# The down-projection in three products begins in block 10 instead of block 11

## The chip, the cores and the metric

The kernel runs on one core of a Trainium2 chip. The metric is the device time of one execution in microseconds (us). TensorE appears in the profile as PE (its weight loads as PEld), VectorE as DVE, ScalarE as ACT, GpSimd as POOL, SyncE as SP.

## The reference

Eight batches of an attention over a packed set of 32 rows, and then one gated feed-forward layer over all 4608 tokens:

```python
p_packed = sm_attn(p, k, v)                # 8 x 8 heads, 576 rows, 64 wide, 32 packed rows
out = sm_attn(q, p_packed, p_packed)
x = out.transpose(0, 2, 1, 3).reshape(4608, 512)
h = x @ w_in                               # 512 -> 2048
g = h * np.tanh(np.log1p(np.exp(h)))       # Mish
return g @ w_out                           # 2048 -> 512
```

## The kernel before

The work runs in blocks `t`, one for each batch `b` (8) and each slice `f` of 128 of the 2048 hidden columns (16), so that blocks 0 to 15 belong to batch 0. A block computes its slice of `h` for the 576 rows of its batch (the up-projection, line 858: twelve matmuls into two PSUM tiles `ps_h`), ACT applies Mish (line 880, and line 882 for the last 64 rows, kept apart in `g_rest`), and the down-projection adds the slice to four accumulators `acc`, one for each chunk `c` of 128 rows. Up to block 16 the down-projection runs one block behind: block `t` multiplies the slice of block `t - 1` (`dn`).

The matmul takes float operands in one call (line 920), which the trace lists as two matmuls per chunk, or operands that are split in two halves, `hi` and `lo`, of another type. Split operands need three products (lines 900 to 902). Which is taken in batch 0 is decided by the constant THREE:

```python
if b == 0 and f < THREE:
    nc.tensor.matmul(out=accs[c], lhsT=grp.act[:, cs], rhs=wo[f], ...)
else:
    down_one(accs[c], grp.g[0], grp.g[1], cs, f, f == 0, f == NF - 1)
```

From slice THREE on, `halves()` splits the activations right after Mish: ACT writes `hi` (line 892), DVE subtracts for `lo` (line 896), into a tile `g_pair`. `split_wo` does the same with a slice of w_out: ACT at line 132, DVE (the function that it returns as `bottom`) at line 135. With the three products a block of batch 0 also puts the down-projection of chunk 1 behind its up-projection; with floats it stands ahead of it.

During batch 0 three other things run beside this. First, the weights arrive as 64-bit words and are turned into floats: ACT (lines 726 and 727, in `words`), POOL (lines 728 and 731, in `words`), then DVE (lines 738 and 742, in `join`). Second, the attention of batch 1 advances a step at a time (`advance(gen)`): in blocks 9 and 10 the values (PE line 585), whose two results DVE normalises at line 292 into `pp`; then PE transposes `pp` (line 596), DVE copies the transpose into `ppT` (line 597), and PE multiplies it with the queries (line 490, called the match here). Third, in every odd block w_in is multiplied with `ppT` of batch 0 for the next two slices (line 757), and ACT and DVE split the product (lines 799 and 800).

What an attention step leaves for DVE is put in a list, `pending`, and written into DVE's order only when the next step begins (`flush`). In blocks 0 to 15 the order on every engine is that of the program; each engine works strictly through its own. From block 16 on a scheduler orders the engines other than PE, PE keeps the program's order.

Of the kernel before, what the change touches and what calls it, by code (L numbers as in the profile page):

```python
# [28 lines left out]
LOADS = {0: 1, 2: 1, 4: 1, 5: 1, 6: 1}  # L29
LATER = 12  # L30
FLOATS = 4
THREE = 11
FIRST_SLOTS = 2
TOGETHER = 2
IN_TURN = 9
# [10 lines left out]
def body(  # L46
# [57 lines left out]
    stg = ctx.enter_context(tc.tile_pool(name="stg", bufs=1, side="right"))  # L104
    KEPT = STB - FIRST_SLOTS - (NF - THREE)

    wo, wo_hi, wo_lo = {}, {}, {}

    def slot(dtype, name, first):
        tag, n = ("st_a", FIRST_SLOTS) if first else ("st_b", STB - FIRST_SLOTS)  # L110
        return stg.tile([P, 2, FC], dtype, name=name, tag=tag, bufs=n)
# [7 lines left out]
    def wo_slot(dtype, name, late):  # L119
        tag, n = ("wo_b", NF - THREE) if late else ("wo_a", THREE + 1)  # L120
        return wts.tile([P, DO], dtype, name=name, tag=tag, bufs=n)

    def split_wo(i, later=False):
        own = STB - (NF - THREE)
        if i >= THREE or i < own:
            pair = slot(F32R, "wo_pair", KEPT <= i < own)
            wo_hi[i], wo_lo[i] = pair[:, 0], pair[:, 1]
        else:
            wo_hi[i], wo_lo[i] = [
                wo_slot(F32R, f"wo_{x}", 2 * (i - own) + n < NF - THREE) for n, x in enumerate(("hi", "lo"))  # L130
            ]
        top = nc.scalar.copy(out=wo_hi[i], in_=wo[i])

        def bottom():
            return nc.vector.tensor_tensor(
                out=wo_lo[i], in0=wo[i], in1=wo_hi[i].bitcast(F32), op=ALU.subtract
            )

        if later:
            return bottom  # L140
        both = [top, bottom()]
        if i < THREE:
            for x in both:
                tc.keep_in_program_order(x)
# [559 lines left out]
    class Weight:  # L704
# [15 lines left out]
        def words(self):  # L720
            x = self.st.rearrange("p m (n t) -> p (m n) t", t=2)
            j, half = divmod(self.at, 2)
            self.r = stg.tile(
                [P, FC], I32, name="wround", tag=f"{('upper', 'lower')[half]}_{j % WB == 0}", bufs=1 if j % WB == 0 else WB - 1
            )
            nc.scalar.activation(out=self.dst, in_=x[:, :, 1].bitcast(F32), func=AF.Copy, scale=F64_SCALE)
            nc.scalar.activation(out=self.r, in_=x[:, :, 0].bitcast(U32), func=AF.Copy, scale=2.0 ** -29)
            nc.gpsimd.tensor_scalar(
                out=self.dst, in0=self.dst, scalar1=F64_HIGH, scalar2=-F64_HIGH, op0=ALU.min, op1=ALU.max
            )  # L730
            nc.gpsimd.tensor_scalar(
                out=self.r.bitcast(BF16).rearrange("p (x t) -> p x t", t=2)[:, :, 1], in0=self.dst,
                scalar1=0.0, scalar2=1.0, op0=ALU.mult, op1=ALU.mult,
            )

        def join(self):
            bits = self.dst.bitcast(I32)
            nc.vector.tensor_scalar(
                out=bits, in0=bits, scalar1=3, scalar2=None, op0=ALU.logical_shift_left,
            )  # L740
            yield
            nc.vector.tensor_tensor(out=bits, in0=bits, in1=self.r, op=ALU.add)
# [77 lines left out]
    def split(*srcs, in_order=False):  # L820

        hi, lo = split_tiles("r")
        for n, src in enumerate(srcs):
            h, l = (x.rearrange("p (f u t) -> p u f t", u=len(srcs), f=src.shape[1])[:, n] for x in (hi, lo))
            both = [
                nc.scalar.copy(out=h, in_=src),
                nc.vector.tensor_tensor(out=l, in0=src, in1=h.bitcast(F32), op=ALU.subtract),
            ]
            if in_order and n == 0:
                for x in both:  # L830
                    tc.keep_in_program_order(x)
        return hi, lo
# [211 lines left out]
    with tc.manual_schedule(engines={mybir.EngineType.PE}):  # L1044
# [57 lines left out]
        for t in range(n_groups + LAG):  # L1102
# [35 lines left out]
            if t == 0:  # L1138
# [10 lines left out]
                ahead.up_floats((0, 1), (1,))  # L1149
                words(6)  # L1150
                join(3)
            if t == THREE:
                bottom()
            elif t == 12:
                split_wo(t)
            if t == 12:
                bottom = split_wo(13, True)
# [74 lines left out]
            if grp:  # L1232
                if t >= NF:
                    grp.halves()
                if t == THREE - 1:
                    bottom = split_wo(THREE, True)
                if t <= 13 and t != 1:
                    words(WORDS.get(t, 2 * t + 9))
            if dn and dn.b % 2 == 1 and dn.f % 4 == 2:
                rest["g"] = split(dn.g_rest[0][dn.f // 4], dn.g_rest[1][dn.f // 4], in_order=(dn.b, dn.f) == (1, 2))  # L1240
            last = dn and dn.b % 2 == 1 and dn.f == NF - 1 and not final
# [49 lines left out]
```

## Time and profile before

| | |
|---|---|
| median of 3 executions | 725.13 us (724.68 to 725.22) |
| profiled execution | 726.51 us, of which the span from first to last instruction 724.8 us |
| PE busy | 714.1 us, 99% of the span |
| DVE, ACT, POOL busy | 424.8, 318.5, 73.6 us |
| granted TensorE clock | 0.996 of full speed (mean) |

The profiled execution has 1.7 us around its span and stands 1.4 us above the median. A busy share is a mean over the whole span: in the page's slices from 18 to 127 us, in which batch 0 runs, DVE is busy for eight to nine tenths.

### The profile page before, as it was taken

What the parts mean: (1) busy time and instruction counts of PE and PEld (TensorE: products, weight loads), DVE (VectorE), ACT (ScalarE), POOL (GpSimd) and SP (SyncE); (2) the same over time, 40 slices, a digit from 0 to 9 for tenths busy, and PEclk for the clock granted to TensorE, in tenths of its full rate; (3) what the DMA queues carried; (4) which work ended last, traced back from release to release, by engine and by line L of the source; (5) the groups of instructions that cost most, each with busy time, mean ns of one, the idle gap of its engine ahead of it and who ended that gap; (6) DMA issues with size and microseconds to landing.
All of it is one profiled execution on the core that took longest, in us unless ns stands there. A gap on an engine that the chain in (4) does not pass through costs nothing.

```text
span 724.8 us, 12806 instructions
## 1 busy us (share of the span) xinstructions
PE 714.1 (99%) x5112; PEld 559.3 (77%) x5112; DVE 424.8 (59%) x765; ACT 318.5 (44%) x719; POOL 73.6 (10%) x105
## 2 busy tenths in 40 slices
PE   8899999999999999999999999999999999999997
PEld 5455568778887788787887888887888878888885
DVE  4888899758636566546645566455574565433322
ACT  4687776545424344254342544342442524432221
POOL 0494832000000000000000000000000000000000
PEclk9999999999999999999999999999999999999999
DMA  9999963651213512235102442133102000010002
GB/s 225 283 297 237 324 105 82 117 97 43 34 45 64 105 33 33 71 61 100 30 5 83 73 91 33 59 63 70 33 1 73 1 2 1 0 59 1 1 1 73
DMA packets 187115, 56.35 MB, mean 78 GB/s; under 512 B 175024, under 2 KB 177328, under 8 KB 187056
## 3 DMA queue, kind: packets, MB, share of 16 engines
q1 hardware_dynamic: 183376, 47.14, 29.5%
q10 hardware_dynamic: 2336, 4.20, 1.6%
q0 software_dynamic: 1344, 4.20, 1.5%
q8 instruction: 40, 0.66, 0.4%
q14 instruction: 19, 0.16, 0.1%
HBM read 46.07 MB, written 9.44 MB: 77 GB/s over the span
## 4 chain that ended last, share of the span: by engine, by line
PE 92%; ACT 3%; DVE 2%; DMA 1%; SPq 1%; issue 1%; POOL 1%; POOLq 0%; DVEq 0%; ACTq 0%
PE ps_h L858 26%; PE acc L900 16%; PE acc L902 15%; PE acc L901 15%; PE ps_w L757 4%; PE acc L920 4%; PE ps_rest L900 2%; PE ps_rest L902 2%; PE ps_rest L901 2%; PE ps_h L490 2%; DMA q_t<-in_q_dram 1%; PE ps_h L569 1%; PE ps_s L490 1%; PE ps_a L549 1%; PE ps_h L870 1%
## 5 line engine op out<-in xcount | busy, mean ns | idle before, releaser
L880 ACT ACTIVATE g<-ps_h 128x256 f32<-128x256 f32 (+2 forms) x256 | 97.3, 384 | 256.6 <-PE ps_h L858 235.1
L858 PE MATMUL ps_h<-aT_hi,wp_hi 128*128 128x256 f32 x496 | 150.7, 304 | 0.0
L858 PE MATMUL ps_h<-aT_lo,wp_hi 128*128 128x256 f32 x496 | 146.6, 295 | 0.0
L858 PE MATMUL ps_h<-aT_hi,wp_lo 128*128 128x256 f32 x496 | 146.4, 295 | 0.0
L895 DVE CAST g_hi<-g 128x512 fp32r<-128x512 f32 x112 | 47.4, 424 | 166.5 <-ACT g L880 166.5
L858 PEld LDWEIGHTS ps_h<-aT_hi,wp_hi 128*128 128x128 f32 x496 | 93.6, 189 | 13.7 <-issue 4.7
L858 PEld LDWEIGHTS ps_h<-aT_lo,wp_hi 128*128 128x128 f32 x496 | 93.5, 189 | 11.0 <-issue 1.9
L858 PEld LDWEIGHTS ps_h<-aT_hi,wp_lo 128*128 128x128 f32 x496 | 93.6, 189 | 0.0
L900 PE MATMUL acc<-wo_hi,g_hi 128*128 128x512 f32 x224 | 90.4, 404 | 0.0
L900 PE MATMUL acc<-wo_pair,g_hi 128*128 128x512 f32 x224 | 89.0, 397 | 0.0
L901 PE MATMUL acc<-wo_lo,g_hi 128*128 128x512 f32 x224 | 88.5, 395 | 0.0
L902 PE MATMUL acc<-wo_pair,g_lo 128*128 128x512 f32 x224 | 88.4, 394 | 0.0
L902 PE MATMUL acc<-wo_hi,g_lo 128*128 128x512 f32 x224 | 88.3, 394 | 0.0
L901 PE MATMUL acc<-wo_pair,g_hi 128*128 128x512 f32 x224 | 88.2, 394 | 0.0
L896 DVE TENSOR_TENSOR g_lo<-g,g_hi 128x512 fp32r<-128x512 f32 x112 | 77.0, 687 | 6.8 <-DVE g_hi L895 0.5
L768 ACT CAST wp_hi<-ps_w 128x512 fp32r<-128x512 f32 x56 | 30.1, 591 | 66.4 <-PE ps_w L757 66.4
L900 PEld LDWEIGHTS acc<-wo_hi,g_hi 128*128 128x128 f32 x224 | 42.2, 189 | 21.1 <-issue 10.9
L900 PEld LDWEIGHTS acc<-wo_pair,g_hi 128*128 128x128 f32 x224 | 42.2, 188 | 10.9 <-issue 3.8
L902 PEld LDWEIGHTS acc<-wo_hi,g_lo 128*128 128x128 f32 x224 | 42.1, 188 | 9.8
L902 PEld LDWEIGHTS acc<-wo_pair,g_lo 128*128 128x128 f32 x224 | 42.1, 188 | 9.7
L901 PEld LDWEIGHTS acc<-wo_lo,g_hi 128*128 128x128 f32 x224 | 42.1, 188 | 4.6
L901 PEld LDWEIGHTS acc<-wo_pair,g_hi 128*128 128x128 f32 x224 | 42.1, 188 | 4.5
(162 smaller groups left out, 982.9 us busy)
## 6 DMA issues: line engine op xcount, KB each, us to landing
w_st<-in_moe_w_in_dram SPq DMA_DIRECT2D x16, 512.0 KB, 7.7
w_st<-in_moe_w_out_dram SPq DMA_DIRECT2D x16, 512.0 KB, 7.0
q_n<-in_q_dram SPq DMA_DIRECT2D x56, 144.0 KB, 3.1
v_n<-in_v_dram SPq DMA_DIRECT2D x56, 128.0 KB, 2.8
k_n<-in_k_dram SPq DMA_DIRECT2D x32, 144.0 KB, 3.1
out_dram<-o ACTq DMA_DIRECT2D x14, 256.0 KB, 2.0
k_n<-in_k_dram SPq DMA_DIRECT2D x96, 32.0 KB, 2.0
out_dram<-o POOLq DMA_DIRECT2D x12, 256.0 KB, 2.5
```

Source lines behind the costliest of these rows:

```text
L490: nc.tensor.matmul(out=ps[u][h * NP:(h + 1) * NP, :], lhsT=packT[u * D:(u + 1) * D, n:n + NP], rhs=xT[u * D:(u + 1) * D, h ^ g, :], start= ...
L549: nc.tensor.transpose(out=ps[:, j, :], in_=flat[:, g, first + j * P:first + (j + 1) * P], identity=ident)
L757: nc.tensor.matmul(out=ps[h * NP:(h + 1) * NP, :], lhsT=ppTb[row:row + D, g, h * NP:(h + 1) * NP], rhs=w[row:row + D], start=True, stop=Tr ...
L768: nc.scalar.copy(out=hi, in_=ps)
L858: nc.tensor.matmul(out=ps, lhsT=w[:, fs], rhs=a[:, g, cs], start=(n == 0), stop=(n == 5))
L880: nc.scalar.activation(out=self.act[:, a:a + m], in_=ps[:, :m], func=AF.Mish)
L895: nc.vector.tensor_copy(out=hi, in_=self.act)
L896: nc.vector.tensor_tensor(out=lo, in0=self.act, in1=hi.bitcast(F32), op=ALU.subtract)
L900: nc.tensor.matmul(out=acc, lhsT=hi[:, cs], rhs=wh, start=start, stop=False)
L901: nc.tensor.matmul(out=acc, lhsT=hi[:, cs], rhs=wl, start=False, stop=False)
L902: nc.tensor.matmul(out=acc, lhsT=lo[:, cs], rhs=wh, start=False, stop=stop)
L920: nc.tensor.matmul(out=accs[c], lhsT=grp.act[:, cs], rhs=wo[f], start=f == 0, stop=f == NF - 1)
```

## The change

THREE goes from 11 to 10, so that slice 10 of batch 0 is multiplied as three products instead of floats. Its w_out slice is split in time for that: the ACT half at the end of block 9, the DVE half at the start of block 10. The same split leaves block 26, where it stood. The activations of block 10 get an ACT copy and a DVE subtraction, and chunk 1 in block 10 moves behind the up-projection. The split of the w_out slice of the block ahead now stands behind `words` instead of ahead of it. Sizes of some rings of buffers follow from THREE (`KEPT`, `wo_slot`, `split_wo`).

```diff
-THREE = 11
+THREE = 10
...
-            if t == THREE:
+            if THREE <= t < 12:
                 bottom()
             elif t == 12:
                 split_wo(t)
...
                 if t >= NF:
                     grp.halves()
-                if t == THREE - 1:
-                    bottom = split_wo(THREE, True)
                 if t <= 13 and t != 1:
                     words(WORDS.get(t, 2 * t + 9))
+                if THREE - 1 <= t < 11:
+                    bottom = split_wo(t + 1, True)
```

On DVE, at the start of block 10 (`wo_797` is slice 10 of w_out, `wo_867` and `wo_870` are slices 11 and 12, `pp` is the normalised result of the attention's values):

```order
 L742 ISA wi_0_98<-wi_0_98,wround 128x1024
 L742 ISA wi_1_99<-wi_1_99,wround 128x1024
-L292 TENSOR_SCALAR pp<-ps_pp,rs 128x128 x2
+L135 TENSOR_TENSOR wo_pair<-wo_797,wo_pair 128x512
+L292 TENSOR_SCALAR pp<-ps_pp,rs 128x128
+L896 TENSOR_TENSOR g_pair<-g,g_pair 128x512
+L292 TENSOR_SCALAR pp<-ps_pp,rs 128x128
 L738 TENSOR_SCALAR wo_867<-wo_867 128x512
 L738 TENSOR_SCALAR wo_870<-wo_870 128x512
```

The second normalisation stood right behind the first; now the subtraction on block 10's activations stands between them. Behind these rows follow, before and after alike, the two joins at line 742 of the same two slices and the two copies into `ppT` at line 597.

On PE, in block 10 (`wo_752` is slice 9 of w_out, `acc_537` to `acc_540` are the four chunks; the row of line 585 is the second group of values). First the place behind the values:

```order
 L920 MATMUL acc_537<-wo_752,g 128x512
 L585 MATMUL ps_pp<-v_n,a1T_n 32x64 x20
+L858 MATMUL ps_h_90<-aT_hi,wp_hi 128x256
+L858 MATMUL ps_h_90<-aT_lo,wp_hi 128x256
+L858 MATMUL ps_h_90<-aT_hi,wp_lo 128x256
```

The up-projection of block 10 (twelve matmuls, three are shown) now follows the values directly; before, chunk 1 (`acc_538`) stood between them and now stands behind the up-projection. Then the end of block 10 and the start of block 11, before:

```order
 L920 MATMUL acc_539<-wo_752,g 128x512
 L596 MATMUL ps_ppT<-ident,pp 128x128 x2
 L920 MATMUL acc_540<-wo_752,g 128x512
-L490 MATMUL ps_s_1148<-xT,ppT 32x288 x4
-L490 MATMUL ps_s_1149<-xT,ppT 32x288 x4
-L920 MATMUL acc_537<-wo_797,g 128x512
```

and with the change, from the match on:

```order
+L490 MATMUL ps_s_1154<-xT,ppT 32x288 x4
+L490 MATMUL ps_s_1155<-xT,ppT 32x288 x4
+L900 MATMUL acc_537<-wo_pair,g_pair 128x512
+L901 MATMUL acc_537<-wo_pair,g_pair 128x512
+L902 MATMUL acc_537<-wo_pair,g_pair 128x512
```

The match keeps its place behind the fourth chunk of slice 9; what follows it, the first chunk of slice 10, is now three matmuls. The order on POOL and SP is the same as before.

## Rows read from the trace of the kernel before

**Rows 1.** The page, busy time, share of the span and instructions of each engine.
```profile
PE 714.1 (99%) x5112; PEld 559.3 (77%) x5112; DVE 424.8 (59%) x765; ACT 318.5 (44%) x719; POOL 73.6 (10%) x105
```

**Rows 2.** Waits of PE from 45 to 719 us (total, times, longest).
```profile
PE ps_pp L585 <- DVE wp_lo L800: 0.4, 1, 0.4
```

**Rows 3.** Chain that ended last, blocks 10 to 12: start, us, what.
```profile
89.16 1.06 PE acc L920 x2
90.22 1.59 PE ps_h L858 x12
...
92.66 0.22 PE ps_ppT L596 x2
...
93.74 0.65 PE ps_s L490 x16
94.39 1.06 PE acc L920 x2
...
97.03 0.86 PE acc L920 x2
97.89 0.59 PE ps_w L757 x16
98.48 1.91 PE acc L920 x4
100.39 0.65 PE ps_s L490 x16
101.04 0.43 PE acc L900
101.47 0.23 PE acc L901
```

**Rows 4.** Timeline of DVE: start, us, what, times [idle before <-releaser].
```profile
85.71 1.69 DVE L738 TENSOR_SCALAR wi<-wi 128x512 int32<-128x512 int32 x2
87.32 2.19 DVE L742 CUSTOM_DVE_ANT_0 wi<-wi,wround 128x1024 uint16<-128x1024 uint16 x2
89.44 0.60 DVE L292 TENSOR_SCALAR pp<-ps_pp,rs 128x128 f32<-128x128 f32 x2
89.96 0.79 DVE L738 TENSOR_SCALAR wo<-wo 128x512 int32<-128x512 int32 x2
90.67 1.28 DVE L742 CUSTOM_DVE_ANT_0 wo<-wo,wround 128x1024 uint16<-128x1024 uint16 x2
92.81 0.49 DVE L597 COPY ppT<-ps_ppT 128x128 f32<-128x128 f32 x2 [0.86 <-PE ps_ppT L596]
```

**Rows 5.** Timeline of DVE, splits in blocks 12 and 13.
```profile
104.75 0.69 DVE L896 TENSOR_TENSOR g_pair<-g,g_pair 128x512 fp32r<-128x512 f32 x1
105.35 0.68 DVE L135 TENSOR_TENSOR wo_pair<-wo,wo_pair 128x512 fp32r<-128x512 f32 x1
...
109.73 1.24 DVE L896 TENSOR_TENSOR g_pair<-g,g_pair 128x512 fp32r<-128x512 f32 x1 [0.64 <-ACT g_pair L892]
```

**Rows 6.** Timeline of ACT, blocks 10 and 13.
```profile
92.22 0.62 ACT L132 CAST wo_pair<-wo 128x512 fp32r<-128x512 f32 x1
92.73 0.68 ACT L726 ACTIVATE wi<-w_st 128x512 f32<-128x512 f32 x1
...
109.08 0.62 ACT L892 CAST g_pair<-g 128x512 fp32r<-128x512 f32 x1
```

**Rows 7.** Timeline of POOL, blocks 9 to 11: last instruction, next after an idle stretch, last.
```profile
89.06 1.08 POOL L731 TENSOR_SCALAR wround<-wo 128x512 bf16<-128x512 f32 x1
93.50 0.61 POOL L728 TENSOR_SCALAR wi<-wi 128x512 f32<-128x512 f32 x1 [3.36 <-ACT wi L726]
...
97.93 1.08 POOL L731 TENSOR_SCALAR wround<-wo 128x512 bf16<-128x512 f32 x1
```

**Rows 8.** Windows: busy us of PE, PEld, DVE, ACT, POOL (instructions), granted clock, DMA share, GB/s.
```profile
20.00:24.00 4.00, 2.33 (x30) 1.46 (x34) 1.83 (x5) 2.95 (x7) 1.72 (x2) 0.86 1.02 395
24.00:44.00 20.00, 19.42 (x86) 9.44 (x75) 15.66 (x26) 15.57 (x32) 13.39 (x16) 0.94 0.95 300
```

## The prediction

> **What bounds the kernel now.** I read the page first: PE is busy for 714.1 of 724.8 us [rows 1]. Since a busy PE is not a PE at its peak, the second view is who PE waits for: from 45 to 719 us it waits once, for 0.4 us, in block 9 [rows 2]. The third is the chain that ended last, which through blocks 10 to 12 is one PE piece after the other, without a gap [rows 3]. So two things follow for any edit behind 45 us. PE work that goes is won in full, and an idle stretch that PE gains is lost in full, because no later wait is there to swallow it. The fourth view is therefore the order of time on DVE, ACT and POOL around block 10 [rows 4 to 7]: what matters there is whether something comes too late for PE.
>
> **The change, part by part.** The sum is made against the profiled execution (726.51 us), and its difference is then put on the median of 725.13 us, which is 1.4 us lower; nothing in the sum depends on that offset.
>
> *PE work.* Slice 10 in floats costs its four chunks 1.06 us (behind the match), 0.86 us and 1.91 us for the last two: 3.83 us [rows 3]. A product of halves takes 0.23 us, the first one behind a match 0.43 us [rows 3]. Twelve products with such a first one in two places (behind the match and, as the float pair of 1.91 us shows with its 0.19 us over 2 x 0.86, behind the weight product of line 757) are 2 x 0.43 + 10 x 0.23 = 3.16 us. PE saves 0.67 us. Moving chunk 1 in block 10 changes no work: the extra 0.2 us that a float chunk pays behind matmuls on parts of the array (1.06 against 0.86 us) is paid by the up-projection instead, for which I take 0.15 us, between 0 and 0.2.
>
> *Split of w_out's slice 10.* One ACT copy and one DVE subtraction go from block 26 to blocks 9 and 10. In block 26 nothing is won, since PE doesn't wait there [rows 2]. A few splits of batch 1 also change places with their neighbours, with the same cover. In block 9 the ACT copy (0.62 us [rows 6]) falls into an idle stretch that ends when the up-projection's results come. On DVE the subtraction comes first in block 10, at 89.44 us; it takes 0.6 us as long as POOL is idle (104.75 to 105.35) and about 1.2 us when POOL works (the 1.24 us row) [rows 5]. POOL works until 90.14 us [rows 7], so I take 0.95 us. It ends at 90.4 us and delays the first normalisation by as much, for which PE has until 92.66 us [rows 3].
>
> *Split of block 10's activations, and what queues behind it.* This is the term that decides. Before, both normalisations ran at 89.44 us, 0.26 us each, and were done at 89.96 us [rows 4]. Now the second stands in DVE's order behind the subtraction of line 896, which needs ACT's copy, which needs Mish, which needs the up-projection. The up-projection starts where chunk 1 stood, at 89.16 instead of 90.22 us, with the 0.15 us above: 0.91 us earlier. The ACT instruction behind Mish started at 92.22 us [rows 6], so the copy for `hi` starts at 91.31 us, takes 0.62 us, and DVE starts 0.03 us after it, as 109.08 + 0.62 against 109.73 us shows [rows 5, 6]: 91.96 us. With 0.60 us for the subtraction and 0.26 us for the normalisation DVE reaches the joins of lines 738 and 742 at 92.82 us, against 89.96 us before: 2.86 us late.
>
> *The four joins.* Between them and PE's match stand two instructions of line 738 and two of line 742, and then the copy into `ppT`. Their price has two values in the trace. With POOL idle they took 89.96 to 91.95 us, 1.99 us; with POOL at work 85.71 to 89.44 us, 3.73 us [rows 4]. Before, they ran in POOL's idle stretch from 90.14 to 93.50 us. Now they don't: ACT's conversion of the next weights starts 0.51 us behind the copy, at 91.82 us, and POOL follows 0.77 us after it (92.73 against 93.50) [rows 6, 7], at 92.6 us, and then works for 5.5 us (93.50 to 99.01) [rows 7]. So I take 3.73 us, with 1.99 us as the other end. The copies into `ppT` start at 96.55 us, the first takes about 0.3 us, and the match starts at about 96.9 us on the scale on which it started at 93.74 us [rows 3].
>
> What the Trainium skill says on this would make it longer: "SBUF — State Buffer", section Who interferes with whom, has DVE and GpSimd hold a shared pair of ports for a whole instruction, the other blocked. Taken strictly, with each of the four behind one POOL instruction of some 0.85 us, that would be 1.99 + 4 x 0.85 = 5.4 us and a match 1.7 us later still. The trace has the same four instructions under an unbroken run of POOL work in 3.73 us, so the row decides, and the strict reading has no more than a part of the 0.04 left for other cases below; it would end at 729.3 us.
>
> *PE at that place.* Values until 89.16, up-projection 1.74, chunks 1 and 2 0.86 each, transposes 0.22 (the second must wait for the normalisation until 92.85 us, some 0.2 us), chunk 3 0.86 us: PE reaches the match at 93.9 us and idles for 3.0 us. The match is 3.16 us late. From there on the saving of 0.67 us is won, and the net is 3.16 - 0.67 = **+2.5 us**, 727.6 us. With the joins at 1.99 us it is +0.75 us.
>
> *What is late next.* DVE is then about as late as PE, and both go on in the same order. The next meeting is the second match (100.39 us before), which needs the splits of line 800. After POOL's work ends (about 98.1 us) DVE's joins run at the short price again, so I count no second wait, and up to 0.4 us for one in the range. Later, slack is as before, since PE and DVE move together.
>
> **The rivals.**
>
> *The clock falls.* An idle stretch of 3.0 us may cost more than itself. In the window from 20 to 24 us PE was busy for only 2.33 of 4 us, and the granted clock fell below full speed in it and behind it: 0.86 there and 0.94 over the next 20 us [rows 8]. That is 0.14 x 4 + 0.06 x 20 = 1.8 us of full-speed clock lost. The same again gives +4.3 us, 729.4 us. Against it: PE is densely busy on both sides of the stretch here, and not there. That a clock falls when PE idles is also what the Trainium skill states ("TensorE: Matmul & The Clock Gate", Part 1); the two levels are 1.2 and 2.4 GHz, and the trace agrees that there is such a fall.
>
> *The joins run at the short price.* If POOL starts later than I count, or the joins slip through between its instructions, the net is +0.75 us, 725.9 us: no difference that a measurement of this kernel can tell, for which I take 0.2%, 1.45 us.
>
> *No wait.* If DVE gets the second normalisation done before it must wait for ACT, or ACT's part is much faster, PE finds `ppT` ready and the change gives its 0.67 us: 724.5 us. It would be won from where the copies into `ppT` start before 93.6 us, less than 0.8 us behind the normalisation at 92.82 us. Four instructions stand there that never took under 1.99 us [rows 4], and an order on DVE that is strict speaks against it. A gain over 0.2% would need 0.8 us more from nowhere that I can see.
>
> **How the numbers follow.** The wait without a fall of the clock: 0.47, own range 726.9 to 728.3 (0.4 us for a second wait, 0.3 us for POOL's and ACT's times either way). With the fall: 0.27, 728.5 to 730.2. Short joins: 0.12. No wait: 0.10. Something else, either side: 0.04. The time given is that of the first. A range from 725.6 to 729.9 us leaves out the case without a wait, part of the short joins and the top of the second, below 0.2 in all. Slower by over 0.2%: 0.76; within: 0.21 (short joins, no wait); faster: 0.03.
>
> **What would show it.** In the changed profile: no PE wait behind 45 us but one of some 3 us at line 490 near 94 us, released by DVE line 597 (the chain passes there from PE to DVE, through lines 738, 742 and 896, and to ACT's line 892); the two joins at some 0.9 to 1.2 us each instead of 0.4 and 0.7; POOL's idle stretch ending about 1 us earlier; twelve matmuls of lines 900 to 902 in block 11, and 3.2 us for them. If the granted clock shows a stretch at half behind 96 us, the first rival holds. I am wrong if PE goes through the match of block 10 without a wait, or if the wait is there and a later one gets shorter by it.

## The result and the profile after

| | before | after |
|---|---|---|
| median, 4 executions each, same chip | 725.17 us (724.68 to 726.56) | 730.11 us (729.93 to 731.85) |
| after/before | | 1.007, 95% interval 1.005 to 1.0091 |
| profiled execution, span | 726.51, 724.8 us | 730.13, 728.4 us |

The change makes the kernel slower by 4.94 us, 0.7%. The prediction was 727.6 us with a range to 729.9 us: the sign was right, the size was too small by 2.5 us, and the result lies 0.2 us above the range.

The page first, as [rows 1] before: busy us, share of the span, instructions of each engine.

```profile
PE 714.3 (98%) x5116; PEld 560.5 (77%) x5116; DVE 425.9 (58%) x766; ACT 319.7 (44%) x720; POOL 74.2 (10%) x105
```

PE has four matmuls more (the floats were 4 chunks of 2, the products are 12), DVE and ACT one instruction more each. Nothing in it tells of 5 us. The waits of PE from 45 to 719 us do, as [rows 2] before: us in total, times, longest.

```profile
PE ps_s L490 <- DVE ppT L597: 2.6, 1, 2.6
PE ps_pp L585 <- DVE wp_lo L800: 0.4, 1, 0.4
PE ps_ppT L596 <- DVE pp L292: 0.3, 1, 0.3
PE ps_w L757 <- DVE wo L738: 0.2, 1, 0.2
```

The second row was there before. The first is the predicted wait, the third the predicted 0.2 us ahead of the transposes; the fourth is new and was not predicted. Now the chain that ended last, through the same blocks as [rows 3]: start, us, what.

```profile
87.13 0.83 PE ps_pp L585 x40
87.96 1.80 PE ps_h L858 x12
89.77 0.02 issue
89.79 0.38 ACT g L880
90.17 0.12 ACT g_rest L882
90.29 0.55 ACT g_pair L892
90.83 0.02 issue
90.86 0.69 DVE g_pair L896
91.55 0.26 DVE pp L292
91.81 1.49 DVE wo L738 x2
93.29 2.12 DVE wo L742 x2
95.42 0.21 DVE ppT L597
95.63 0.04 issue
95.67 1.38 PE ps_s L490 x16
97.06 0.72 PE acc L900
97.78 0.43 PE acc L901
...
103.43 0.65 PE ps_s L490 x16
```

Before, all of this was PE. Now the chain leaves PE behind the up-projection, goes through ACT's Mish and copy to DVE's subtraction, the second normalisation and the four joins, and comes back to PE at the match: 5.9 us of it, from 89.77 to 95.67 us, are not PE's. The rows behind the idle stretch show something else. The match takes 1.38 us and a product 0.43 us; before they took 0.65 and 0.23 us [rows 3]. The windows of PE say why (length, busy us of PE, PEld, DVE, ACT, POOL with instructions, granted clock, DMA share, GB/s):

```profile
20.00:24.00 4.00, 2.65 (x31) 1.41 (x32) 2.91 (x7) 3.48 (x10) 2.02 (x3) 1.00 1.04 394
...
88.00:96.00 8.00, 5.09 (x28) 2.94 (x36) 6.84 (x12) 5.45 (x11) 5.06 (x7) 0.99 0.53 84
96.00:99.00 3.00, 3.00 (x22) 1.79 (x14) 2.93 (x7) 0.00 (x0) 0.80 (x1) 0.50 0.35 55
99.00:104.00 5.00, 5.00 (x52) 3.18 (x50) 2.98 (x6) 3.48 (x9) 0.69 (x2) 0.98 1.08 172
```

From 96 to 99 us the granted clock is 0.50, the lower of the two levels, 1.2 GHz, right behind the stretch in which PE stood idle; then it is back. The fall that the kernel before showed from 20 to 24 us (0.86, [rows 8]) is not there in this execution.

DVE around the wait, as [rows 4] before (start, us, what, times, idle before), and POOL, as [rows 7]:

```profile
88.24 1.20 DVE L135 TENSOR_TENSOR wo_pair<-wo,wo_pair 128x512 fp32r<-128x512 f32 x1
89.36 0.34 DVE L292 TENSOR_SCALAR pp<-ps_pp,rs 128x128 f32<-128x128 f32 x1
90.86 0.69 DVE L896 TENSOR_TENSOR g_pair<-g,g_pair 128x512 fp32r<-128x512 f32 x1 [1.16 <-ACT g_pair L892]
91.47 0.34 DVE L292 TENSOR_SCALAR pp<-ps_pp,rs 128x128 f32<-128x128 f32 x1
91.73 1.57 DVE L738 TENSOR_SCALAR wo<-wo 128x512 int32<-128x512 int32 x2
93.22 2.20 DVE L742 CUSTOM_DVE_ANT_0 wo<-wo,wround 128x1024 uint16<-128x1024 uint16 x2
95.34 0.47 DVE L597 COPY ppT<-ps_ppT 128x128 f32<-128x128 f32 x2
```

```profile
91.48 0.61 POOL L728 TENSOR_SCALAR wi<-wi 128x512 f32<-128x512 f32 x1 [2.53 <-ACT wi L726]
```

DVE is idle for 1.16 us ahead of the subtraction with a normalisation ready behind it; then POOL starts at 91.48 us, and the joins take 91.73 to 95.34 us, 3.61 us against 1.99 us before.

**How executions are compared.** The second group of values (line 585 in block 10) starts between 86.35 and 89.27 us in the thirteen profiled executions, in kernels with the change and without it alike. Most of that scatter is there early: PE's weight product (line 757) near 45 us starts between 45.06 and 47.23 us. From there to the group it is 41.24 to 42.20 us. All of this lies ahead of block 10's match, so I count from the start of this group: to the match, and to the second match, at which the change's work is over. Before, this row of the chain is the start:

```profile
88.33 0.83 PE ps_pp L585 x40
```

PE's timeline, from which the numbers are taken, has starts up to 0.07 us earlier than the chain: 88.26, 93.67 and 100.33 us before, 87.06, 95.67 and 103.36 us after. So, to 0.01 us, the match comes 5.41 us behind the values before and 8.61 us after, the second match 12.06 and 16.30 us; I call the second number the stretch. These numbers repeat to 0.1 us where kernels have the same work there and the clock doesn't fall, and from the second match to PE's last matmul it is 618.9 to 619.5 us in all kernels but one. So the stretch explains 4.24 us of the difference.

### The profile page after: what moved, and what is told of

Same layout as the page of the kernel before. It is cut to its first block, busy times and chain, and to the rows that moved or that the text cites. A ratio compares the mean times of both kernels' runs of the same rounds, so it can differ in the third digit from the quotient of the medians.

```text
span 728.4 us, 12816 instructions
## 1 busy us (share of the span) xinstructions
PE 714.3 (98%) x5116; PEld 560.5 (77%) x5116; DVE 425.9 (58%) x766; ACT 319.7 (44%) x720; POOL 74.2 (10%) x105
## 4 chain that ended last, share of the span: by engine, by line
PE 90%; DVE 5%; ACT 3%; POOL 1%; issue 1%; DVEq 0%; POOLq 0%; ACTq 0%
PE ps_h L858 26%; PE acc L900 16%; PE acc L902 15%; PE acc L901 15%; PE ps_w L757 4%; PE ps_rest L900 2%; PE ps_rest L902 2%; PE ps_rest L901 2%; PE ps_h L490 2%; PE ps_h L569 1%; PE ps_s L490 1%; PE acc L920 1%; PE ps_a L549 1%; PE ps_h L1002 1%; DVE wo L742 1%
```

## The experiments

All are compared in this table; the single runs follow. "Match" and "second match" are us from the start of the values in the profiled execution. Times are medians, "before" is the kernel before on the same chips.

| kernel | match | second match | time (before) | ratio, interval |
|---|---|---|---|---|
| before | 5.41 | 12.06 | | |
| after | 8.61 | 16.30 | 730.11 (725.17) | 1.007, 1.005 to 1.0091 |
| after_again | 8.61 | 14.80 | 730.83 (725.33) | 1.0073, 1.0059 to 1.0087 |
| sub_behind | 5.42 | 12.15 | 726.19 (725.39) | 1.0011, 1.0001 to 1.002 |
| norm_first | 7.96 | 15.66 | 729.49 (725.39) | 1.0053, 1.0037 to 1.007 |
| filled | 8.62 | 14.80 | 729.34 (725.39) | 1.0052, 1.0037 to 1.0067 |
| words_late | 6.88 | 13.74 | 727.40 (725.39) | 1.0027, 1.0016 to 1.0038 |
| relieved | 5.41 | 11.82 | 727.09 (725.33) | 1.0022, 1.0013 to 1.0031 |
| split_unused | 6.88 | 13.72 | 727.76 (725.33) | 1.0032, 1.0021 to 1.0044 |
| unused_words | 8.62 | 15.45 | 729.29 (725.11) | 1.0059, 1.0043 to 1.0074 |
| pp_on_act | 5.42 | 11.84 | 725.78 (725.11) | 1.0007, 0.9998 to 1.0016 |
| chunk_moved | 5.41 | 12.07 | 725.66, one execution | |
| words_only | 5.42 | 12.11 | 726.20, one execution | |

**sub_behind: the subtraction for block 10 behind the normalisations and the joins.** In the changed kernel, `halves` hands the subtraction back, and it is written where the block ends:

```diff
-                    grp.halves()
+                    lower = grp.halves(t == 10)
...
                 if t == 10:
+                    lower()
                     join(28)
```

> The changed kernel, but DVE's subtraction on block 10's activations stands behind the two copies into ppT instead of between the two normalisations; ACT's copy stays. If the order on DVE makes the wait at the match of block 10, the normalisations and joins run early as before, PE goes through that match without a wait and the clock doesn't fall there. What is left by the simple theory is the 0.67 us of PE work saved: 724.5 us. By a stricter count DVE has only 0.86 us of idle time in blocks 10 and 11 and is given two more instructions of 0.6 to 1.2 us, so it comes 1 to 1.6 us late to the weight product of line 757 or to the second match, and the result is 725.2 to 726.5 us with a PE wait there. If the added work itself and not its place is the cause, it stays near 730 us.

The wait at the match is gone, and the clock doesn't fall between 45 and 719 us. So the place of the subtraction in DVE's order is what makes the wait: with all other work of the change in place the match comes at 5.42 us. Yet the stretch is no shorter than before. Its chain (columns as above; the products have other line numbers here, the subtraction of block 11 is line 900):

```profile
97.02 1.07 PE ps_w L757 x16
98.09 0.64 ACT wp_hi L799 x2
98.78 0.69 DVE g_pair L900
99.46 0.34 DVE wp_lo L800
99.85 1.02 PE ps_s L490 x16
```

The weight product takes 1.07 instead of 0.59 us [rows 3]: some of its weight loads wait until 97.33 us for DVE's line 608, which takes the result of the match out of PSUM.

```profile
97.33 0.18 PEld L757 LDWEIGHTS ps_w<-wi,ppT 64*32 64x32 f32 x14 [0.23 <-DVE a L608]
```

PE then waits 0.3 us at the second match for line 800, which stands behind a subtraction on DVE. The two eat the 0.65 us that the products save (unused_words, below).

**norm_first: both normalisations ahead of the subtraction.** In the changed kernel:

```diff
                 grp.up(1)
+                if t == 10:
+                    flush()
                 if t < NF:
```

> The changed kernel, but both normalisations stand ahead of the subtraction on block 10's activations; the joins stay behind it. If what PE waits for is the whole queue behind the subtraction, only the 0.26 us of one normalisation are won at the match: the wait at line 490 is still 2.5 to 3 us, the clock still falls, and the time is 729.4 to 730.0 us. If the normalisation alone was held up, the wait goes and the time is 724.5 to 725.2 us.

The match comes at 7.96 us, 0.65 us earlier than after, and PE waits 2.5 us for line 597. The normalisation is 0.26 us of this; the rest is that the first pair of joins, now earlier against POOL (which starts at 92.41 us), takes 1.18 us instead of 1.57 us:

```profile
92.39 1.18 DVE L738 TENSOR_SCALAR wo<-wo 128x512 int32<-128x512 int32 x2
```

So the second normalisation is a small part; what counts is that the four joins and the copies behind them queue behind the subtraction. The clock falls here too (columns as above), but later: PE is busy again from 95.94 us, and the granted clock is still 1.00 up to 97 us.

```profile
97.00:98.00 1.00, 1.00 (x6) 0.87 (x6) 1.00 (x2) 0.00 (x0) 0.92 (x2) 0.87 0.33 50
98.00:101.00 3.00, 3.00 (x13) 2.90 (x12) 2.48 (x5) 0.89 (x4) 0.24 (x1) 0.50 0.58 92
```

**filled: PE kept busy in the idle stretch.** Two more matmul calls with zeros, 128x512 each (the trace lists them as four matmuls), into the tile `ps_h`, whose contents nobody reads any more at that point:

```diff
             elif b == 0 and (not chunk or f >= 11):
+                if t == 10:
+                    warm(8)
                 advance(gen)
```

> The changed kernel, with two matmul calls of zeros (128 x 512 floats, 0.86 us each, into a PSUM tile that nothing reads) in front of the match of block 10, where PE is idle. They are extra work that the result doesn't use. The match starts when it did, since DVE decides. If the half clock behind the idle stretch is part of the loss, PE is busy for two thirds of the stretch, the clock stays at full, and 1.7 us come back: 728.4 us, with PE at 0.23 us for each product in block 11. If the loss is the wait alone and what follows it, the time stays at 730.1 us.

The match comes at 8.62 us as after, with a wait of 0.9 us left, and the stretch is 1.50 us shorter than after; the median, 729.34 us, is not the 728.4 us that I expected. The windows (columns as above):

```profile
90.00:96.00 6.00, 4.84 (x13) 1.77 (x11) 4.83 (x9) 5.08 (x10) 3.84 (x5) 1.00 0.46 72
96.00:99.00 3.00, 2.97 (x30) 2.34 (x31) 2.97 (x7) 0.38 (x1) 1.07 (x2) 1.00 0.39 62
```

Where after did 22 matmuls from 96 to 99 us at 0.50, this one does 30 at 1.00. So the fall costs 1.50 us. Whether it was the filling that kept it away, this run alone doesn't show (after_again, next).

**after_again: the changed kernel once more, on another chip.**

> The changed kernel once more, for a second trace on another chip state and more executions: the wait of 2.6 us at line 490 and a stretch of half clock behind it again, 16.3 us from the second values to the second match, and a time 4.2 to 5.0 us above the kernel before. If the fall of the clock depends on where the idle stretch happens to lie, it is missing here or in some executions, which then lie 1.7 us lower.

The wait of 2.6 us is the same. The clock did not fall behind it, against the first of my two expectations, and the time is 5.50 us above before, where at most 5.0 us were expected:

```profile
20.00:29.00 9.00, 7.36 (x41) 3.71 (x42) 6.15 (x11) 6.16 (x12) 4.33 (x5) 0.62 1.03 390
...
90.00:98.00 8.00, 5.09 (x32) 2.89 (x30) 6.84 (x12) 5.46 (x11) 5.09 (x6) 1.00 0.40 63
98.00:101.00 3.00, 3.00 (x31) 2.35 (x29) 2.97 (x7) 0.39 (x1) 0.92 (x2) 1.00 0.39 62
```

So an idle stretch of the same length is followed by a fall in one execution and not in another. The stretch is 14.80 us, as with filled: wait and saving without a fall are worth 2.74 us. Its profiled execution still took 730.88 us, for it has a longer fall early on, 0.38 x 9 = 3.4 us of full-speed clock lost from 20 to 29 us, where the profile of before lost 1.8 us.

**words_late: the conversion of the next weights behind the attention step.** In the changed kernel, block 10's `words(31)` moves to the end of the block, so that POOL starts later:

```diff
-                if t <= 13 and t != 1:
+                if t <= 13 and t not in (1, 10):
                     words(WORDS.get(t, 2 * t + 9))
...
                     join(28)
+                    words(31)
```

> The changed kernel, but ACT's and POOL's conversion of the next three weight pieces in block 10 comes after the joins of that block, so that POOL is idle while DVE runs them. If POOL's work makes the joins long, the four take 2.0 us instead of 3.6, the match comes 1.6 us later than in the kernel before instead of 3.25, the clock doesn't fall, and the time is 725.6 to 727.0 us. If the joins are long for another reason, the time stays near 730 us.

DVE and POOL in it:

```profile
91.72 0.75 DVE L738 TENSOR_SCALAR wo<-wo 128x512 int32<-128x512 int32 x2
92.39 1.28 DVE L742 CUSTOM_DVE_ANT_0 wo<-wo,wround 128x1024 uint16<-128x1024 uint16 x2
93.59 0.48 DVE L597 COPY ppT<-ps_ppT 128x128 f32<-128x128 f32 x2
```

```profile
94.38 0.61 POOL L728 TENSOR_SCALAR wi<-wi 128x512 f32<-128x512 f32 x1 [5.44 <-ACT wi L726]
```

With POOL behind them the same joins take 1.87 us, and the match comes at 6.88 us. So of its 3.20 us of lateness 1.73 us are POOL's work beside the joins and 1.47 us the queue. The kernel is not as fast as expected, because POOL's work now lies beside DVE's next work (line 135 takes 1.20 instead of 0.68 us, line 896 1.20 instead of 0.69 us): PE waits 0.4 us at line 757 and 0.6 us at the second match, where after has 0.2 us and nothing. That is why short joins gave +1.68 us and not the +0.75 us of my second rival.

**relieved: sub_behind with two joins later, numbers 28 and 29 of the conversions.**

```diff
-... 10: 25, 11: 29, 14: 32}
+... 10: 25, 11: 28, 14: 32}
...
-                    if t in (5, 9, 13):
-                        join({5: 15, 9: 25, 13: 31}[t])
+                    if t in (5, 9, 11, 13):
+                        join({5: 15, 9: 25, 11: 29, 13: 31}[t])
...
                     lower()
-                    join(28)
```

> The kernel with the subtraction behind the copies into ppT, and in addition the joins of two weight pieces that nobody needs before blocks 12 and 13 come one step later on DVE: that of the w_out slice 13 from the end of block 10 into block 11, that of a w_in piece from the middle of block 11 to behind the splits of line 800. If DVE's lack of room in blocks 10 and 11 is what ate the 0.67 us, PE passes line 757 and the second match without a wait, the stretch from the second values to the second match takes 11.4 us against 12.06 us in the kernel before, and the time is 0.3 to 0.7 us below the kernel before (724.5 to 725.1 us). If the saving of PE work isn't real, the stretch stays at 12.0 us or more.

The stretch is 0.24 us shorter than before, the only gain but that of pp_on_act, and it is lost again later: behind the second match PE takes 620.46 us, 0.9 to 1.5 us more than elsewhere. The longest wait of PE from 45 to 719 us:

```profile
PE acc L906 <- DVE g_pair L900: 0.7, 1, 0.7
```

In this kernel line 906 is the third product and line 900 the subtraction for `lo`; the wait is in block 13. My expectation of a gain in the time was wrong: I took DVE to have room in the blocks behind, and it has too little up to block 13.

**chunk_moved, words_only: one part of the change alone.** On the kernel before, chunk 1 of block 10 behind the up-projection (`THREE - 1 <= t < NF` as the condition of its two places), or the split of w_out behind `words`:

```diff
-                if t == THREE - 1:
-                    bottom = split_wo(THREE, True)
                 if t <= 13 and t != 1:
                     words(WORDS.get(t, 2 * t + 9))
+                if t == THREE - 1:
+                    bottom = split_wo(THREE, True)
```

> The kernel before, with chunk 1 of block 10 behind the up-projection as the only difference. No work is added and nothing waits for the moved matmuls: the stretch from the second values to the second match takes 12.0 to 12.2 us as before. If the move itself lets PE reach the match too early or too late, it is longer by 0.5 us or more.

> The kernel before, with the ACT half of slice 11's split behind the weight conversion in block 10 as the only difference. POOL starts 0.5 us earlier, but the joins are done by then: the stretch takes 12.0 to 12.2 us. If the early POOL work hurts by itself, the stretch is longer by 0.5 us or more.

Neither does anything to the stretch (12.07 and 12.11 us).

**split_unused, unused_words: the activations are split, but slice 10 is still multiplied in floats.** Nobody reads the halves, so the result is complete. The first is chunk_moved with the split, the second has the split of w_out behind `words` as well:

```diff
-                if self.f < THREE:
+                if self.f < THREE - 1:
                     return
```

> The kernel before, with chunk 1 of block 10 behind the up-projection and with the two instructions that split block 10's activations, whose result is not used: slice 10 is still multiplied in floats and its w_out slice is split where it was. If the queue on DVE behind the subtraction makes the loss, the wait of some 2.5 to 3 us at the match and the half clock behind it are there without any of the three products, and the 0.67 us are missing on top: the stretch from the second values to the second match takes 16.5 to 17.1 us, the time is 730.2 to 731.4 us. If the three products or the split of w_out make the loss, the time stays within 1 us of the kernel before.

> The kernel before with chunk 1 of block 10 behind the up-projection and the unused split of block 10's activations, as in the run that came out at a stretch of 13.72 us, and now also with the ACT half of slice 11's split behind the weight conversion instead of ahead of it, as the change has it. Ahead of it, that ACT copy waits for DVE's joins and so holds POOL's work off them; behind it, POOL works while DVE joins. If that is why the four joins cost 1.87 us there and 3.6 us in the changed kernel, the stretch grows to 15.5 us, or to 17.0 us where the clock falls, and the time is 729.5 to 731.4 us, without any of the three products. If the three products have a part in the long joins, the stretch stays near 13.7 us and the time near 727.8 us.

The first came out 3 us shorter than I expected. Its ACT shows why; then DVE and POOL of the second:

```profile
93.39 0.62 ACT L132 CAST wo_pair<-wo 128x512 fp32r<-128x512 f32 x1 [2.29 <-DVE wo L742]
```

```profile
92.02 1.58 DVE L738 TENSOR_SCALAR wo<-wo 128x512 int32<-128x512 int32 x2
93.52 2.20 DVE L742 CUSTOM_DVE_ANT_0 wo<-wo,wround 128x1024 uint16<-128x1024 uint16 x2
95.64 0.48 DVE L597 COPY ppT<-ps_ppT 128x128 f32<-128x128 f32 x2
...
91.79 0.61 POOL L728 TENSOR_SCALAR wi<-wi 128x512 f32<-128x512 f32 x1 [2.56 <-ACT wi L726]
```

In split_unused ACT's copy for slice 11 stands ahead of `words`. It waits 2.29 us for DVE's joins, and with it all of ACT's conversions, and so POOL: the joins run alone and take 1.87 us. With the order of the change ACT goes on to `words`, POOL starts at 91.79 us, and the joins take 3.62 us. So the third edit of the change, which alone does nothing, is what lets POOL's work onto the joins here (1.73 us), and with it makes PE's idle stretch as long as it is. Against after_again, unused_words differs on PE by the multiplications alone: 15.45 less 14.80 us, 0.65 us for twelve products instead of four float chunks.

**pp_on_act: the second way round the queue.** In the changed kernel, ACT does batch 1's normalisations, the joins stand ahead of the subtraction, and in block 10 the split of w_out is ahead of `words` again:

```diff
+                nc.scalar.activation(
+                    out=self.pp[g], in_=pp_ps.unsqueeze(1).to_broadcast([P, 2, D]), func=AF.Copy,
+                    scale=self.rs[:, g:g + 1],
+                )
...
+                if t == 10:
+                    flush()
+                    join(27)
                 if t < NF:
...
+                if t == 10:
+                    bottom = split_wo(11, True)
                 if t <= 13 and t != 1:
                     words(WORDS.get(t, 2 * t + 9))
-                if THREE - 1 <= t < 11:
-                    bottom = split_wo(t + 1, True)
+                if t == 9:
+                    bottom = split_wo(10, True)
```

> The changed kernel with DVE's queue in block 10 made short: both normalisations go to ACT, the four joins stand ahead of the subtraction, and the ACT half of slice 11's split stands ahead of the weight conversion again. DVE then has 0.5 us less to do. If DVE's queue is all that keeps the 0.67 us from being won, the stretch takes 11.4 to 11.8 us and the time is 0 to 0.5 us below the kernel before (724.8 to 725.4 us). If something else costs as much, the stretch stays at 12.1 us or more.

The match comes at 5.42 us, the second one at 11.84 us, 0.22 us before the kernel before's: of the 0.65 us saved, 0.3 us go to a wait at the second match (for line 806, the line 800 of before). In the time it can't be told from no change, where I expected up to 0.5 us of gain, and no kernel here beats the one before.

## Why the prediction was wrong, step by step

**What bounds the kernel.** Right: an idle stretch of PE behind 45 us was lost in full. Behind the second match PE's 619.06 us became 619.24 us.

**PE work.** Right: 0.67 us predicted, 0.65 us measured. Moving chunk 1 cost nothing (chunk_moved), as taken. The split of w_out's slice 10 on DVE took 1.20 us instead of 0.95 us, and cost nothing.

**The queue on DVE.** Right, and in its sum closer than in its parts, which is luck: two errors cancel. From the values' start the copy for `hi` was predicted at 91.31 - 88.33 = 2.98 us and came at 90.29 - 87.13 = 3.16 us; the joins took 3.61 us, where I took 3.73 us and kept 1.99 us as the other end; the match was 3.20 us late, predicted 3.16 us. PE's waits of 2.6 and 0.3 us stand for the 3.0 and 0.2 us. The net of wait and saving was +2.74 us (after_again, filled), predicted +2.5 us. What I did not see is why POOL comes beside the joins: I had the time of ACT's conversion from the copy for `hi`, but not that it is the third edit that puts it there.

**"What is late next": I counted no second wait.** Off by a little: 0.2 us (after) and 0.4 us (after_again) at line 757. This is what the +2.74 has over the +2.5.

**"The wait without a fall of the clock: 0.47".** This is the step that failed. I set the fall at 0.27, on the ground that PE is densely busy on both sides of the stretch, and so the time given holds nothing for it. PE is busy there, and the clock fell to 0.50 all the same, in the profiled execution of after (96 to 99 us) and in that of norm_first (98 to 101 us); in after_again and unused_words, with a wait of 2.6 us too, it did not. So of four profiles with a wait of 2.5 or 2.6 us two have the fall, and of the nine others none has it there: dense work around the stretch was no protection. The price of the rival, 1.8 us, was near the 1.50 us measured, and the rival's range, 728.5 to 730.2 us, holds the result. The Trainium skill states in "TensorE: Matmul & The Clock Gate", Part 1, that a PE left idle gets the lower clock. The traces of after and norm_first agree, with 0.50 behind the idle stretch; those of after_again and unused_words show 1.00 behind it.

**The top of the range.** 729.9 us leaves no room for what the stretch doesn't explain: 4.94 - 4.24 = 0.70 us. In the two profiles 0.18 us of that lies behind the second match and 0.38 us behind PE's last matmul (5.8 against 5.4 us), and the latter is 5.8 us in words_only too, whose stretch is that of before; so I can't tie it to the change. The result is 2.5 us above the time given: 1.50 us for the fall, 0.24 us for the net of wait and saving, and these 0.70 us. It takes both the fall and the open 0.70 us to leave the range.

**What stays open.** What decides whether the clock falls in an execution; I saw it in one profile of two of the same kernel, and the mean clocks of the unprofiled executions (0.993 to 0.997) don't tell where a fall lay; that the median of after holds a fall is therefore inferred from its profiled execution, not shown. And the remainder: in every kernel that was timed more than once, the median is further above before than the profiled stretch explains, by 0.3 to 1.2 us (filled, without a fall: 3.95 us, of which the stretch is 2.74 us), by 2.0 us in relieved and by 2.8 us in after_again. It is 0.8 us in split_unused and unused_words too, where slice 10 is multiplied in floats, so the three products alone don't make it.

**The joins beside POOL.** The Trainium skill, "SBUF — State Buffer", section Who interferes with whom, has a DVE instruction that uses the ports shared with GpSimd exclude the other engine for the whole instruction. My strict reading of it, each join behind one whole POOL instruction, was an estimate of 5.4 us. The trace disagrees with that sum: 3.61 us beside POOL, 1.87 us without. Which of the joins use the shared ports no run here shows.

## What to carry to other kernels

Before a new instruction that waits for another engine goes into a strict queue, read what stands behind it: here a subtraction of 0.69 us that stood idle for 1.16 us held back four conversions and, behind them, the copies that PE needed, and 0.65 us of saved matmuls became 4.9 us of loss. A long wait on one queue can also be what keeps two engines apart: when ACT's copy no longer waited, POOL's work fell on DVE's joins and made them 1.73 us longer, so look at what an instruction that comes free now runs beside. And where PE gains an idle stretch like the one here, a wait of 2.5 or 2.6 us, put the fall of the clock into the sum as a chance, even amid dense work: two of four profiles had it, for 1.50 us.

## What the hardware showed unexpectedly

- Of two profiled executions of the same kernel with the same idle stretch (wait of 2.6 us at line 490), one has the clock at 0.50 for 3 us behind it, the other at 1.00. In norm_first the fall came over 1 us after PE was busy again.
- The four joins take 1.87 us alone and 3.62 us beside POOL, twice over: 0.75 and 1.58 us for the pair at line 738, 1.28 and 2.20 us for the pair at line 742.
